# More of the start-up masks and all diagonal fills on GpSimd, the weight check moved behind the weights: a recurrent attention and its MLP on one core

## The chip, the cores and the metric

One core of one Trainium2 chip runs the kernel. The metric is the device time of one execution in microseconds (us). TensorE is called PE (PEld is its weight load), VectorE DVE, ScalarE ACT, GpSimd POOL and SyncE SP.

## The reference

There are 4 batches, 8 heads, 768 positions and a head size of 48. For each head a 48×48 state runs along the positions:

```python
cur = einsum('bhd,bhe->bhde', u[None] * kt, vt)
y[:, :, t] = einsum('bhd,bhde->bhe', rt, state + cur)
state = w[None, :, :, None] * state + einsum('bhd,bhe->bhde', kt, vt)
```

The outputs of all heads stand side by side as x (3072 tokens × 384) and go through an MLP of width 2048:

```python
h = x @ w_in
g = np.maximum(h, 0.0) + alpha * np.minimum(h, 0.0)
return g @ w_out
```

All inputs and the output are float32.

## The kernel before

**Tiling.** The positions are cut into 6 chunks of 128, so that a chunk has 512 tokens over the batches. Two heads make a pair, on partitions 0 to 47 and 64 to 111; there are 4 pairs. Inside a chunk the recurrence is written as products: r and k are scaled by tables of powers of w, scores are k against r under a strict triangular mask, the diagonal holds u·k·r, and what came before the chunk enters through the state. The MLP goes in main-loop steps: one step is one tile of 128 hidden columns of one chunk. `m_in` (L734) makes the hidden tile from x with 9 products (weights and x are each split into a high and a low float32r part, and three of the four combinations are taken, over 3 blocks of x), ACT and DVE make the activation and split it, and `m_out` (L760), 3 steps later, adds 9 products to the three output accumulators. There are 96 steps: 9 of chunk 0, 9 of chunk 1, the other 7 of each, then 16 of each later chunk.

**Start-up.** PE first runs 19 bf16 products on the identity (`warm`, L832 and L836), before any data is there. `first_chunk` (L437) handles the four pairs q of chunk 0, with tiles of the full 128 positions: DVE scales r and k (L447), makes their product (L533), PE sums it with u into the diagonal (`c_sum`, L540) and makes the scores (L457), DVE weighs v with the diagonal (L464), the scores are masked into `below`, and PE forms y (L485, L489, L498), which ACT copies out as the high part of x, PE subtracts (L508) and ACT copies again as the low part (L504). The mask of head g = 1 of a pair is a copy by ACT (L471) and a select by POOL (`affine_select`, L473); that of g = 0 is a DVE copy under a predicate (L477) onto a tile that POOL has cleared once (L268). The powers come from DVE (`table`, L275 to L279; L279 squares the last power into `w128`). `tokens_table` (L311) turns them into a table by tokens, `whalf`: ACT writes rows (L315), PE turns them (L322), DVE copies them (L325). With it DVE scales k of chunk 0 (L431) for the states (L521).

**Weights.** Each of the 16 weight tiles is loaded by SP (L334) and split by ACT and DVE (L359 to L378); the low part `wl` (L378) comes last, and a step needs both parts.

**Later chunks.** `burst` (L607) does a pair of chunks 1 to 5 with tiles of 64 positions: it makes scores and state products for one pair (L626, L633) and y for the pair before (L652 through the state, L662 through the scores). `prepare` (L553) loads and scales. There the tile `base` first gets the diagonal value `cu` on a 64×64 identity, for each of 2 heads and 4 batches (8 instructions per pair: in chunk 1 by POOL, L594, after that by ACT, L598), and then DVE copies the scores over it above the diagonal (L681). For chunks 2 to 5 `cu` comes from two POOL products (L582, L584) and a DVE sum (L588); for chunk 1 from PE (L540) and ACT (L546). L717 and L722 split y of chunk 1 by ACT and PE; L405 and L406 do it by ACT and DVE later.

**The check.** `check` (L808) tests that alpha is at most 1 and w lies within bounds, on DVE (L814 to L820), PE (L823) and DVE again (L825 to L829), and writes a flag that chooses, at the end, a general path which does not run here. Its rank is 40. All engines load the flag (L887).

**What sets the order.** Every instruction or small group is a `Piece` with an engine, a cost in us that is written into the code, the tiles that it reads and writes, and a rank. `in_order` (L93) plays the engines against these costs and picks, on the engine that is free first, the ready piece of the lowest rank; the resulting order is fixed when the program is built, and each engine runs its part strictly in that order. Scores, y and hidden tiles take turns in five PSUM banks, given out in that play. Where PE is idle in it ahead of the first step, filler `warm` products are written in front of the piece (L872 to L884). An SP load is costed by a shared transfer rate (L166).

## Time and profile before

| | |
|---|---|
| Three runs | 484.70, 484.49 and 485.74 us, median 484.7 us |
| The profiled execution | 485.77 us, of which the span from first to last instruction is 483.7 us |
| Granted TensorE clock, mean | 0.998 of full speed |
| DVE, ACT, POOL busy | 309.9, 244.8 and 98.4 us |
| Loaded from HBM | 37.17 MB |

Times in the views count from the start of the span. An engine's row gives the line of the code, the operation, the tiles written and read, and the count; a bracket tells how long the engine was idle before it and what ended that. PE's products are pipelined, so the busy time of one row runs into the next.

### The profile page before, as it was taken

The numbers are of one execution on the slowest core, as the hardware profiler recorded it, in microseconds if no ns is written. First come the engines' busy times: TensorE is split into PE (matmuls) and PEld (weight loads), VectorE is DVE, ScalarE is ACT, GpSimd is POOL, SyncE is SP. The second block draws the span as 40 slices with busy tenths as digits, with TensorE's granted clock in tenths as the row PEclk, the third lists the DMA queues.
The fourth block names the chain that finished last, engine by engine and source line by source line (L and its number), as shares of the span: only waits on it lengthen the run. The fifth ranks groups of instructions, "written<-read, shape, count | busy, mean of one in ns | idle before, by whom it ended". The sixth has DMA issues, their size and how long they took to land.

```text
span 483.7 us, 11271 instructions
## 1 busy us (share of the span) xinstructions
PE 473.4 (98%) x4667; PEld 385.5 (80%) x4667; DVE 309.9 (64%) x519; ACT 244.8 (51%) x554; POOL 98.4 (20%) x119
## 2 busy tenths in 40 slices
...
GB/s 220 284 228 184 250 248 170 214 147 51 54 160 122 211 96 59 149 88 37 88 54 37 151 89 35 72 56 1 119 1 1 1 1 0 66 0 1 0 0 71
DMA packets 23113, 46.22 MB, mean 96 GB/s; under 512 B 3376, under 2 KB 11184, under 8 KB 23056
## 3 DMA queue, kind: packets, MB, share of 16 engines
...
q8 instruction: 38, 0.62, 0.5%
q10 hardware_dynamic: 128, 0.23, 0.2%
q14 instruction: 19, 0.16, 0.1%
HBM read 37.17 MB, written 6.29 MB: 90 GB/s over the span
## 4 chain that ended last, share of the span: by engine, by line
PE 86%; DVE 5%; POOL 4%; ACT 2%; DMA 2%; issue 1%; ACTq 0%; DVEq 0%
PE acc L774 40%; PE bank L740 38%; POOL base L594 4%; PE bank L652 2%; PE bank L662 2%; PE bank L633 2%; PE bank L626 1%; DMA raw<-rk 1%; DVE raw L447 1%; ACT x L717 1%; DVE raw L565 1%; DMA wp<-wP 1%; DVE wl L378 1%; DVE kk L431 0%; DVE g L533 0%
## 5 line engine op out<-in xcount | busy, mean ns | idle before, releaser
L740 PE MATMUL bank<-x,wh 128*128 128x512 f32 x576 | 195.3, 392 | 0.0
L749 DVE SCALAR_TENSOR_TENSOR g<-bank,alph,g 128x512 f32<-128x512 f32 x96 | 71.9, 749 | 106.6 <-ACT g L748 106.5
L740 PEld LDWEIGHTS bank<-x,wh 128*128 128x128 f32 x576 | 108.1, 188 | 24.0 <-issue 0.8
L748 ACT ACTIVATE g<-bank 128x512 f32<-128x512 f32 x96 | 57.2, 596 | 129.2 <-PE bank L740 128.8
L740 PE MATMUL bank<-x,wl 128*128 128x512 f32 x288 | 112.2, 389 | 0.0
L752 ACT ACTIVATE gh<-g 128x512 fp32r<-128x512 f32 x96 | 60.5, 630 | 72.2 <-DVE g L749 72.1
L753 DVE TENSOR_TENSOR gl<-g,gh 128x512 fp32r<-128x512 f32 x96 | 72.4, 754 | 36.9 <-ACT gh L752 36.8
L774 PE MATMUL acc<-gh,wh 128*128 128x512 f32 x288 | 83.2, 396 | 0.0
L774 PE MATMUL acc<-gh,wl 128*128 128x512 f32 x288 | 81.6, 390 | 0.0
L774 PE MATMUL acc<-gl,wh 128*128 128x512 f32 x288 | 81.5, 390 | 0.0
L774 PEld LDWEIGHTS acc<-gh,wl 128*128 128x128 f32 x288 | 53.9, 188 | 11.4
L774 PEld LDWEIGHTS acc<-gl,wh 128*128 128x128 f32 x288 | 53.9, 188 | 11.3
L740 PEld LDWEIGHTS bank<-x,wl 128*128 128x128 f32 x288 | 54.1, 188 | 10.8
L774 PEld LDWEIGHTS acc<-gh,wh 128*128 128x128 f32 x288 | 52.7, 188 | 11.6 <-issue 0.4
L582 POOL TENSOR_TENSOR rr<-rr,kk 128x384 f32<-128x384 f32 x16 | 22.3, 1393 | 161.4 <-DMA kk<-vkr 93.6
L598 ACT ACTIVATE base<-ident,cu 128x64 f32<-128x64 f32 x128 | 32.9, 337 | 1.7 <-DVE cu L588 1.7
L594 POOL TENSOR_SCALAR base<-ident,cu 128x64 f32<-128x64 f32 x32 | 30.8, 984 | 13.7 <-ACT cu L546 13.7
L390 POOL DMA_DIRECT2D x<-x x30 | 15.4, 519 | 61.3 <-ACT o L801 49.4
L406 DVE TENSOR_TENSOR x<-bank,x 48x256 fp32r<-48x256 f32 x64 | 27.0, 422 | 1.3
L405 ACT ACTIVATE x<-bank 48x256 fp32r<-48x256 f32 x64 | 24.2, 379 | 2.1 <-PE bank L662 1.0
L568 DVE TENSOR_TENSOR raw<-raw,W 112x512 f32<-112x512 f32 x32 | 22.4, 723 | 2.2 <-DMA raw<-rk 2.2
L584 POOL TENSOR_TENSOR rr<-rr,utab 128x384 f32<-128x384 f32 x16 | 22.5, 1408 | 1.2
...
## 6 DMA issues: line engine op xcount, KB each, us to landing
...
```

The lines of the kernel that those rows point to most:

```text
L405: add("ACT", us, lambda: nc.scalar.activation(h(), view(), AF.Copy), r=[src], w=parts(x, 0, ps), rank=rank)
L406: add("DVE", us + 0.1, lambda: nc.vector.tensor_tensor(out=l(), in0=view(), in1=h(), op=ALU.subtract), r=[src] + parts(x, 0, ps), w=parts( ...
L568: add("DVE", 0.72, lambda t=t, tab=tab: nc.vector.tensor_tensor(out=t().rearrange("p b (j t) -> p (b j) t", j=2), in0=t().rearrange("p b ( ...
L584: add("POOL", 1.2, lambda: nc.gpsimd.tensor_tensor(out=rt().rearrange("p (g b) e -> p g b e", g=2), in0=rt().rearrange("p (g b) e -> p g b ...
L594: add("POOL", 1.0, lambda g=g, b=b: nc.gpsimd.tensor_scalar(base()[:, g, b], ident2(), cu()[:, g, b:b + 1], None, op0=ALU.mult), r=[cu, id ...
L598: add("ACT", 0.32, lambda g=g, b=b: nc.scalar.activation(base()[:, g, b], ident2(), AF.Copy, scale=cu()[:, g, b:b + 1]), r=[cu, ident2], w ...
L740: nc.tensor.matmul(hp()[:, :], a[i]()[:, k], X[c]()[:, x, k], start=(k == 0 and j == 0), stop=(k == NK - 1 and j == 2))
L748: add("ACT", 0.6, lambda: nc.scalar.activation(g(), hp()[:, :], AF.Copy), r=[hp], w=[g], rank=n - 100)
L749: add("DVE", 0.75, lambda: nc.vector.scalar_tensor_tensor(out=g(), in0=hp()[:, :], scalar=alph()[:, i:i + 1], in1=g(), op0=ALU.mult, op1=A ...
L752: add("ACT", 0.64, lambda: nc.scalar.activation(gh(), g(), AF.Copy), r=[g], w=[gh], rank=n - 100)
L753: add("DVE", 0.73, lambda: nc.vector.tensor_tensor(out=gl(), in0=g(), in1=gh(), op=ALU.subtract), r=[g, gh], w=[gl], rank=n - 99)
L774: nc.tensor.matmul(banks[k](), a[i]()[:, NK + k], x(), start=(begin and j == 0), stop=(end and j == 2))
```

## The change

The planner costs SP loads of under 16 KB at a fixed time, out of the shared rate. The masks of g = 0 for pairs 0 and 1 are done as those of g = 1, with a copy by ACT and a select by POOL, so the two clears of `below` go. The square of the last power moves from DVE to POOL. The first turn of the table by tokens gets rank −93 in place of −45. The diagonal of `base` is written, for all pairs of chunks 1 to 5, by two POOL selects, one for each half of the partitions: it takes the value of `cu`, read with step 0 along the position, where row and column agree, and 0 elsewhere. The check gets rank 24, and its first two DVE instructions name the last weight tile as an input. 22 warm products are written, and no filler follows directly behind them.

```diff
@@ -164,8 +164,11 @@
             if e == "POOL" and p.kb:
                 p.end += 3.0
             if e == "SP" or p.kb and e == "ACT":
-                dma = max(dma, p.end + 1.5) + p.kb / DMA_RATE
-                p.end = dma + 0.3
+                if p.kb < 16:
+                    p.end += 1.7
+                else:
+                    dma = max(dma, p.end + 1.5) + p.kb / DMA_RATE
+                    p.end = dma + 0.3
             done.append(p)
             for q in heirs.get(p, ()):
                 left[q] -= 1
@@ -263,9 +266,6 @@
     add("POOL", 0.1, lambda: nc.gpsimd.memset(uw(), 0.0), w=[uw], rank=-98)
     for i in range(2):
         add("POOL", 0.4, lambda i=i: nc.gpsimd.memset(weighed[i](), 0.0), w=[weighed[i]], rank=-95 + i)
-        for g in range(2):
-            if g == 0:
-                add("POOL", 0.4, lambda i=i, g=g: nc.gpsimd.memset(below[i][g](), 0.0), w=[below[i][g]], rank=-95 + i)
     for g in range(2):
         add("POOL", 0.25, lambda g=g: nc.gpsimd.tensor_tensor(
             out=uw()[half(g), :, g], in0=up()[half(g)], in1=wp()[half(g)], op=ALU.mult),
@@ -276,7 +276,7 @@
             out=t()[:, 64:129], data0=a()[:, m:m + 1].broadcast_to([112, 65]), data1=unit(), initial=0.0,
             op0=ALU.mult, op1=ALU.add), r=[wp, unit], w=[t], rank=10 * m - 95)
         add("DVE", 0.55, lambda: nc.vector.reciprocal(t()[:, 0:64], t()[:, 128:64:-1]), w=[t], rank=10 * m - 95)
-        add("DVE", 0.1, lambda: nc.vector.tensor_tensor(
+        add("POOL", 0.25, lambda: nc.gpsimd.tensor_tensor(
             out=w128()[:, m:m + 1], in0=t()[:, 128:129], in1=t()[:, 128:129], op=ALU.mult), r=[t], w=[(w128, m)],
             rank=10 * m - 78)
 
@@ -321,7 +321,7 @@
             for m in range(P):
                 nc.tensor.transpose(pt()[0:n, 128 * m:128 * m + 112], rows()[:, m, 0:n], ident()[0:112, 0:112])
 
-        add("PE", 0.6, turn, r=[rows, ident], w=[pt], rank=at)
+        add("PE", 0.6, turn, r=[rows, ident], w=[pt], rank=at - 48 * first)
         add("DVE", 0.4, lambda: nc.vector.tensor_copy(
             whalf()[0:n].rearrange("p (m g) e -> p m g e", g=2),
             pt()[0:n, :].rearrange("p (m g e) -> p m g e", m=P, g=2)[:, :, :, 0:D]), r=[pt], w=[whalf], rank=at)
@@ -467,12 +467,12 @@
             in1=bank()[:, 8 * q:8 * q + 8].rearrange("p (b g) -> p g b", g=2)[:, :, :, None].broadcast_to([128, 2, B, D]),
             op=ALU.mult), r=[(bank, q), v], w=[vc], rank=10 * q - 77)
         for g in range(2):
-            if g and True:
-                add("ACT", 0.6, lambda: nc.scalar.activation(
-                    base[1]().rearrange("p b t -> p (b t)"), A[1]()[:, :], AF.Copy), r=[A[1]], w=[base[1]], rank=q - 94)
-                add("POOL", 1.6, lambda: nc.gpsimd.affine_select(
-                    base[1](), base[1](), pattern=[[0, B], [1, L]], base=0, channel_multiplier=-1,
-                    compare_op=ALU.is_gt, fill=0.0), w=[base[1]], rank=q - 94)
+            if g or q < 2:
+                add("ACT", 0.6, lambda g=g: nc.scalar.activation(
+                    base[g]().rearrange("p b t -> p (b t)"), A[g]()[:, :], AF.Copy), r=[A[g]], w=[base[g]], rank=q - 94)
+                add("POOL", 0.75, lambda g=g: nc.gpsimd.affine_select(
+                    base[g](), base[g](), pattern=[[0, B], [1, L]], base=0, channel_multiplier=-1,
+                    compare_op=ALU.is_gt, fill=0.0), w=[base[g]], rank=q - 94)
                 continue
             add("DVE", 0.75, lambda g=g: nc.vector.copy_predicated(
                 base[g](), strict()[:, None, :].broadcast_to([128, B, L]),
@@ -588,16 +588,13 @@
             add("DVE", 0.55, lambda: nc.vector.tensor_reduce(
                 out=cu().rearrange("p g b -> p (g b)"), in_=rt(), axis=AX.X, op=ALU.add), r=[rt], w=[cu], rank=at - 1.8)
         base = sb([128, 2, B, HI], "base", 3)
-        for g in range(2):
-            for b in range(B):
-                if hasty:
-                    add("POOL", 1.0, lambda g=g, b=b: nc.gpsimd.tensor_scalar(
-                        base()[:, g, b], ident2(), cu()[:, g, b:b + 1], None, op0=ALU.mult), r=[cu, ident2],
-                        w=[(base, (g, b))], rank=at - 0.9)
-                    continue
-                add("ACT", 0.32, lambda g=g, b=b: nc.scalar.activation(
-                    base()[:, g, b], ident2(), AF.Copy, scale=cu()[:, g, b:b + 1]), r=[cu, ident2],
-                    w=[(base, (g, b))], rank=at - 0.9)
+        for j in range(2):
+            rows = slice(HI * j, HI * (j + 1))
+            add("POOL", 0.75, lambda rows=rows: nc.gpsimd.affine_select(
+                base()[rows].rearrange("p g b t -> p (g b) t"),
+                cu()[rows].rearrange("p g b -> p (g b)")[:, :, None].broadcast_to([HI, 2 * B, HI]),
+                pattern=[[0, 2 * B], [1, HI]], base=0, channel_multiplier=-1, compare_op=ALU.is_equal, fill=0.0),
+                r=[cu], w=[base], rank=at - 0.9)
         if hasty:
             by_tokens(k0, k, at - 3, at - 1.6)
         else:
@@ -809,11 +806,11 @@
 
         ok, w2, total = sb([128, NF + P + 1], "ok", 1), sb([112, P], "w2", 1), plan.buf(lambda: ok()[0:1, NF + P:])
         count = psum()
-        at = 40
+        at = 24
         add("POOL", 0.1, lambda: (ok(), w2(), nc.gpsimd.memset(ok()[:, 0:NF + P], 0.0)), w=[ok], rank=at)
-        add("DVE", 0.1, lambda: nc.vector.tensor_scalar(ok()[:, 0:NF], alph(), 1.0, None, op0=ALU.is_le), r=[alph],
+        add("DVE", 0.1, lambda: nc.vector.tensor_scalar(ok()[:, 0:NF], alph(), 1.0, None, op0=ALU.is_le), r=[alph, wl[NF - 1]],
             w=[ok], rank=at)
-        add("DVE", 0.1, lambda: nc.vector.tensor_tensor(out=w2(), in0=wp(), in1=wp(), op=ALU.mult), r=[wp], w=[w2],
+        add("DVE", 0.1, lambda: nc.vector.tensor_tensor(out=w2(), in0=wp(), in1=wp(), op=ALU.mult), r=[wp, wl[NF - 1]], w=[w2],
             rank=at)
         add("DVE", 0.1, lambda: nc.vector.tensor_scalar(ok()[0:112, NF:NF + P], w2(), 0.75 ** 2, None, op0=ALU.is_ge),
             r=[w2], w=[ok], rank=at)
@@ -833,7 +830,7 @@
         x = ident().bitcast(mybir.dt.bfloat16)
         nc.tensor.matmul(bank()[:, 256:512], x[:, 0:128], x, start=True, stop=True, skip_group_check=True)
 
-    add("PE", 4.0, lambda: [warm() for _ in range(19)], r=[ident], w=[(bank, "warm")], rank=-1000)
+    add("PE", 4.7, lambda: [warm() for _ in range(22)], r=[ident], w=[(bank, "warm")], rank=-1000)
 
     begins = {}
     for n, (c, i) in enumerate(STEPS):
@@ -856,7 +853,7 @@
     for n in range(NM):
         jobs.append((n, 6, lambda n=n: m_in(n)))
         jobs.append((n + MLAG - 0.5, 5, lambda n=n: m_out(n)))
-    jobs.append((40, 7, check))
+    jobs.append((24, 7, check))
 
     for m in range(P):
         table(m)
@@ -876,7 +873,8 @@
             if any(x is acc_of[0] for x, _ in p.uses):
                 break
             step = p.rank >= 0 and p.us == 0.7
-            fill[p], last = 0 if last is None else int(max(0.0, p.start - last - 0.05) / (0.25 if step else 0.125)), p.end
+            fill[p] = 0 if last is None else int(max(0.0, p.start - last - 0.05) / (0.25 if step else 0.125))
+            last = p.end if p.rank > -1000 else None
     with tc.manual_schedule():
         for p in order:
             for _ in range(fill.get(p, 0)):
```

## Rows read from the trace of the kernel before

**Rows 1.** The page, part 1: busy time and share of the span of each engine
```profile
PE 473.4 (98%) x4667; PEld 385.5 (80%) x4667; DVE 309.9 (64%) x519; ACT 244.8 (51%) x554; POOL 98.4 (20%) x119
```

**Rows 2.** Windows: length; busy us PE, PEld, DVE, ACT, POOL; clock, DMA share, GB/s
```profile
15.00:20.00 5.00, 5.00 (x72) 3.88 (x71) 4.93 (x12) 5.00 (x15) 1.00 (x2) 1.00 1.05 350
40.00:45.00 5.00, 4.66 (x114) 3.73 (x115) 4.66 (x10) 2.73 (x6) 5.00 (x5) 1.00 0.48 135
100.00:150.00 50.00, 50.00 (x517) 41.27 (x516) 42.73 (x68) 29.89 (x77) 13.10 (x10) 1.00 0.38 119
```

**Rows 3.** Chain that ended last, first 100 us, two pieces: start, us, what
```profile
33.96 9.16 POOL base L594 x8
53.56 8.38 POOL base L594 x8
```

**Rows 4.** Waits of PE, 26 to 81 us, all of them: total, times, longest
```profile
PE bank L652 <- ACT x L717: 0.7, 1, 0.7
PE bank L652 <- DVE base L681: 0.3, 1, 0.3
PE bank L540 <- DVE g L533: 0.2, 1, 0.2
PE bank L303 <- DVE raw L565: 0.2, 1, 0.2
```

**Rows 5.** Timeline of PE, to 31 us: start, us, line, op, tiles, count, idle before
```profile
1.46 5.09 PE L834 MATMUL acc<-ident 128*128 128x256 bf16 x23 [1.46 <-POOL ident L249]
13.25 1.16 PE L457 MATMUL bank<-raw 48*128 48x128 f32 x16 [0.19 <-DVE raw L447]
23.37 0.74 PE L498 MATMUL bank<-x,pick 112*128 112x512 f32 x2
26.06 0.48 PE L740 MATMUL bank<-x,wh 128*128 128x512 f32 x1
30.69 0.82 PE L834 MATMUL acc<-ident 128*128 128x256 bf16 x6
```

**Rows 6.** Timeline of DVE, 8 to 42 us, chosen rows
```profile
8.85 1.14 DVE L533 TENSOR_TENSOR g<-raw 112x512 f32<-112x512 f32 x1
10.38 0.73 DVE L477 COPY_PREDICATED below<-strict,bank 128x512 f32<-128x512 uint8 x1
11.90 1.29 DVE L447 TENSOR_TENSOR raw<-raw,W 112x512 f32<-112x512 f32 x2
13.11 0.15 DVE L279 TENSOR_TENSOR w<-W 112x1 f32<-112x1 f32 x1
...
21.99 0.17 DVE L814 TENSOR_SCALAR ok<-alph 128x16 f32<-128x16 f32 x1
...
30.70 0.95 DVE L378 TENSOR_TENSOR wl<-wx,wh 128x768 fp32r<-128x768 f32 x1
41.49 0.16 DVE L825 TENSOR_REDUCE ok<-bank 1x1 f32<-1x20 f32 x1
```

**Rows 7.** Timeline of POOL, 8.8 us
```profile
8.81 0.64 POOL L473 TENSOR_SCALAR_AFFINE_SELECT below<-below 128x512 f32<-128x512 f32 x1 [2.78 <-ACT below L471]
```

**Rows 8.** Instructions of one line: ns shortest/median/longest, first and last start
```profile
L533 DVE TENSOR_TENSOR g<-raw x7: 683/693/1137, 6.0 to 54.4; 112x512 f32<-112x512 f32 x7
L594 POOL TENSOR_SCALAR base<-ident,cu x32: 433/442/4077, 34.0 to 66.1; 128x64 f32<-128x64 f32 x32
```

**Rows 9.** Groups by line: count | busy us, mean ns of one | idle before
```profile
L598 ACT ACTIVATE base<-ident,cu 128x64 f32<-128x64 f32 x128 | 32.9, 337 | 1.7 <-DVE cu L588 1.7
L471 ACT ACTIVATE gl<-acc 128x512 f32<-128x512 f32 x2 | 1.2, 592 | 1.8 <-PE acc L457 1.8
L473 POOL TENSOR_SCALAR_AFFINE_SELECT below<-below 128x512 f32<-128x512 f32 x2 | 1.3, 636 | 6.2 <-ACT below L471 6.2
```

**Rows 10.** Waits of DVE, 26 to 81 us, the longest one
```profile
DVE base L681 <- POOL base L594: 1.6, 4, 0.8
```

**Rows 11.** The flag's load on SP, by its line: ns, first and last start
```profile
L887 SPq TENSOR_LOAD <-flag x1: 492/492/492, 42.5 to 42.5; - x1
```

## The prediction

> **What bounds the kernel now.** I read the page's busy shares first: PE is busy 98% of the span [rows 1], and in the windows it fills its stretch completely from 100 us on (50.00 of 50 us) while DVE has room (42.73) [rows 2]. So behind the start-up the end is set by the length of PE's queue, and work taken from ACT or POOL there buys nothing. The chain that ended last tells another story for the first 100 us: two blocks of POOL's diagonal fills (L594), 9.16 and 8.38 us, stand in it [rows 3]. Those 17.5 us are not to be had. The chain follows the releaser that came last, also while PE has other work in its queue: in the list of what PE waited for between 26 and 81 us there are 1.4 us in all, 0.7 + 0.3 of them at L652, the first products of a burst, behind those fills [rows 4]. Over that stretch PE does main-loop steps as the weights come, attention bursts in between, and filler products.
>
> Before 26.06 us, where the first main-loop product starts [rows 5], DVE is the busiest of the vector engines (4.93 of 5 us at 15 to 20 us, and still 4.66 at 40 to 45) [rows 2]. PE's third scores product at 13.25 us waits for DVE's scaling of r and k that starts at 11.90 [rows 5, 6]; after that PE is full up to the last of x at 23.37 us (5.00 of 5) [rows 2, 5], and then comes a fixed tail of two copies by ACT and one correction by PE up to 26.06. So time is won in three places alone: an earlier 13.25, PE's waits and fillers between 26 and 81 us, or that tail.
>
> **The change, part by part.** Sums are made against the profiled execution (485.77 us, span 483.7); the median of the three runs, 484.7, lies 1.1 us lower, so I apply the difference to the median.
>
> *Masks of pairs 0 and 1.* Two selective copies by DVE (0.73 each, L477) [rows 6] go; ACT gets two copies (0.59 each) and POOL two selects (0.64 each) more [rows 9] (the first select, at 8.81 us, found POOL idle for 2.78 us [rows 7]). Removed from DVE: 2 × 0.73 = 1.46 us, of which one lies ahead of the scaling at 11.90. Two 0.5 us clears of POOL in the first 4 us go with them; nothing waited for those.
>
> *Square of the last power (L279).* Four times 0.15 us leave DVE [rows 6] for POOL, whose small instructions stand behind at most two selects; first users are ACT's rows for the table. 0.6 us of DVE removed, one or two of the four ahead of 11.90 or the next scaling.
>
> *Check behind the weights.* Four small instructions at 21.99 us (at most 4 × 0.17 = 0.68) and three at 41.49 (3 × 0.16 = 0.48) [rows 6] leave the full stretch for some 130 us, where DVE has 7 us of room in 50 [rows 2]; if that room were gone they would cost 1.2 us of DVE, not of PE. Between the two groups the check also holds one of the five rotating PSUM banks, until 41.49 us; that is freed. The flag's load sits in SP's queue right behind the check (42.5 us, 0.49 us) [rows 11] and moves with it; queued behind it on SP are input loads for bursts, which the code ranks seven main-loop steps ahead of their burst, so a wait of a few us there stays hidden, and PE would be the one to wait if not.
>
> *Table turned early.* The transposes get a rank ahead of the remaining first-chunk products. Neither they nor the copy and the four scalings of k behind them get shorter; they come sooner, so the state products can fill the tail ahead of 26.06. But the turn stands in PE's in-order queue: if ACT's rows for it are late, the x products behind it wait. Bounds: from −0.5 (wait) to +0.5 us (the filler and idle time of the tail).
>
> *Warm-up.* 23 products ran at the start, 19 written and 4 as filler, in 5.09 us, 0.22 each [rows 5]; 22 remain, as the filler behind them goes. At most 0.2 us of PE, ahead of a DVE-paced stretch: I take 0.
>
> These four together move the first main-loop product: DVE is eased by 0.73 + 0.15 us ahead of 11.90, but the new selects can take some back, see below. I take 0.5 us, bounds −0.5 and +1.2.
>
> *Diagonal fills of chunk 1.* Eight POOL instructions per pair become two selects. An L594 takes 0.44 us at the median but up to 4.08 [rows 8], and eight took 8.4 to 9.2 us [rows 3]. A fill reads a broadcast column and writes 512 numbers per partition, on half the partitions; the nearest row is the 512-element select at 0.64 [rows 9], upper bound the excess that L594 shows per piece on top: (9.16 − 8 × 0.44) / 8 = 0.7, so 1.3 each. A pair takes 1.3 to 2.7 us in place of 8 to 9. That removes the two waits of PE at L652 and 1.6 us in which DVE stood idle for the fills [rows 10]. Gain on PE: 1.0, bounds 0 (the 0.7 is released by a copy of ACT, which may be late for its own reasons) and 1.4, all of PE's waits.
>
> *Filler and weights.* At 30.69 us PE runs six filler products, 0.82 us [rows 5], and then waits 0.2 for DVE [rows 4]; the second weight tile is only finished by DVE at 31.65 (30.70 + 0.95) [rows 6]. DVE ahead by some 2 us (1.46 + 0.6 + 0.68 = 2.7, less collisions) has it done as the first step ends. Gain 0.6, bounds 0 and 1.1: the fillers are written from the planner's gaps, not from the chip's.
>
> *Diagonal fills of later chunks.* 128 ACT instructions (32.9 us in total) [rows 9] become 32 selects, 20.5 us on POOL at 0.64. POOL is at 13.10 of 50 us there [rows 2]. A select waits for its pair's reduction; queued behind it are the next pair's two POOL products and DMA issues, and the next burst needs the mask about four steps later. At 0, bounds −0.3 and +0.3; if POOL's cover were gone, one late mask would cost PE its wait per burst.
>
> The planner's new price for small loads only reorders them; 0. Sum: 0.5 + 1.0 + 0.6 = 2.1 us: 483.7 for that execution, **482.6** against the median. All lower ends together give 0.8 us lost, all upper ends 4.0 won.
>
> **Row against rule.** DVE's product at 8.85 us took 1.14 us where its kind takes 0.69, and a select had started on POOL 0.04 us before [rows 6 to 8]: 0.44 lost. The other way round, L594's longest pieces stand in full DVE stretches. The Trainium skill, SBUF — State Buffer, section "Who interferes with whom", says that a DVE instruction with two SBUF inputs and a GpSimd instruction that reads SBUF exclude each other for a whole instruction, whoever starts first. The trace agrees with that in this one pair of rows. By it, a select costs DVE up to its full length; by the row 0.44 us, and only where it meets such an instruction.
>
> **The rivals.** *The selects take back what they free.* Ten new selects (two masks, eight fills) run in the stretch where DVE is full. If each blocks a two-input instruction for its whole 0.64 us, DVE loses 6.4 us against 1.46 + 0.6 + 0.68 + 0.48 + 1.6 = 4.8 freed; the weights come 1.6 us later and PE, which starts each of the first steps as its weights arrive, with them: 484.7 + 1.6 = 486.3. It decides from the eighth collision on (4.8 / 0.64 = 7.5). For it: the row at 8.85. Against it: at 0.44 ten collisions cost 4.4, and the 32 instructions that go collided too. The rule above is what this rival rests on.
>
> *Little moves.* The selects of pair 1 fall on the scaling at 11.90, so that the first step stays at 26.06; the 0.7 us wait for ACT remains; gain 0.3 + 0.6 = 0.9: 483.8. For it: PE's queue was full in nearly the whole stretch, so a shorter chain beside it counts for nothing.
>
> *All covers fall at once.* With the bank freed and DVE ahead, the planner packs first chunk and first steps tightly and every term reaches its upper end: 4.0 won, 480.7. Against it: each of these is a separate wait.
>
> **How the numbers follow.** About 0.3% (1.45 us) can be told from no change. The forecast (1.5 to 3.3 us won) gets 0.55, the upper ends 0.07, little moves 0.27, the selects taking it back 0.11. So faster 0.62, same 0.27, slower 0.11. The range goes from 480.6, the upper ends, to 485.3, just short of the lower ends together (485.5); it leaves out the blocking rival's full price and a little at either side.
>
> **What would show it.** Right: the first L740 at 25 to 26 us; no filler near 30 us; PE's waits between 26 and 81 us below 0.5 us; the fills at L594 as selects of 0.6 to 1.3 us and gone from the chain; ACT some 33 us less busy with no gain behind 100 us, where the distance between steps stays as it was. Wrong: selects over 2 us each, two-input DVE instructions of over 1 us around them with the weights' last step (L378) later than now, PE waiting at the turned table or at L489, SP standing long at the flag's load, or new waits at L662 in the later bursts.

## The result, and the profile after

The changed kernel takes 487.79 us (median of 8 runs, 485.59 to 490.27) against 484.93 us (8 runs, 484.49 to 485.74) in the same runs: ratio 1.0058, 95% interval 1.0034 to 1.0081, so 2.9 us slower. (Ratios leave out runs far above a kernel's fastest, which the medians below keep, so that a ratio can differ from the quotient of two medians.) The profiled execution happens to be the fastest of the eight: 485.59 us, span 483.5, against 485.77 and 483.7 before. So the best run of the changed kernel is set beside a run at the slow end of the kernel before. Two facts already lie in these numbers: the best run is 0.7 us above the median of the kernel before and inside its range, and the others lie up to 4.7 us above that best run.

The page, part 1, answers to [rows 1]:

```profile
PE 471.3 (97%) x4650; PEld 383.7 (79%) x4650; DVE 306.5 (63%) x513; ACT 215.9 (45%) x428; POOL 110.2 (23%) x131
```

ACT has lost 28.9 us, POOL has got 11.8 and DVE lost 3.4, as the change says. None of it is time won, so I followed PE instead: the start of the n-th main-loop product (L740 and L774 before, L737 and L771 after, 1728 in all) in the one trace minus that in the other.

| product | before, us | after, us | difference |
|---|---|---|---|
| 1st | 26.06 | 26.18 | +0.1 |
| 217th | 97.85 | 94.77 | -3.1 |
| 352nd | 131.83 | 131.76 | -0.1 |
| last | | | +0.3 |

So 3.1 us were won in the start-up, more than the 2.1 forecast, kept up to 126 us and lost again within 5 us. The waits of PE from 26 to 81 us, all of them, answer to [rows 4], where they were 1.4 us:

```profile
PE bank L649 <- ACT cu L546: 0.2, 1, 0.2
```

And those from 100 to 160 us, where the kernel before has none:

```profile
PE bank L649 <- DVE g L746: 1.7, 1, 1.7
PE bank L659 <- ACT seen_y L672: 0.8, 1, 0.8
```

That is 2.5 of the 3.0 us lost there. The timeline of PE shows where (start, us, line, tiles, count, idle before):

```profile
126.77 0.32 PE L649 MATMUL bank<-raw,T 48*48 48x64 f32 x4
128.76 0.59 PE L649 MATMUL bank<-raw,T 48*48 48x64 f32 x26 [1.67 <-DVE g L746]
...
131.38 0.44 PE L659 MATMUL bank<-base,v 64*48 64x64 f32 x16 [0.81 <-ACT seen_y L672]
```

PE stands in the middle of an attention burst, for the PSUM bank that L746 is to read out. (L746 is DVE's part of the activation g; the expectations call it the accumulation, and so does this text.) The timeline of DVE at that place, after:

```profile
125.29 0.69 DVE L750 TENSOR_TENSOR gl<-g,gh 128x512 fp32r<-128x512 f32 x1 [0.70 <-ACT gh L749]
127.48 0.56 DVE L431 TENSOR_TENSOR kk<-kk,whalf 128x384 f32<-128x384 f32 x1 [1.50 <-POOL rr L582]
127.96 0.74 DVE L746 SCALAR_TENSOR_TENSOR g<-bank,alph,g 128x512 f32<-128x512 f32 x1
```

and the same instructions before (L749 is the accumulation there):

```profile
126.91 0.69 DVE L753 TENSOR_TENSOR gl<-g,gh 128x512 fp32r<-128x512 f32 x1 [0.70 <-ACT gh L752]
127.52 0.74 DVE L749 SCALAR_TENSOR_TENSOR g<-bank,alph,g 128x512 f32<-128x512 f32 x1
129.11 0.56 DVE L431 TENSOR_TENSOR kk<-kk,whalf 128x384 f32<-128x384 f32 x1 [0.84 <-POOL rr L582]
```

The planner has written the two in the other order. Before, the accumulation stood ahead of the scaling of k (L431), and DVE's wait for POOL's product rr fell behind it; now DVE stands 1.50 us for POOL with the accumulation that PE needs queued behind. Why is POOL's rr not 3.1 us earlier too, as PE is? The timeline of POOL after:

```profile
100.00 4.50 POOL L593 TENSOR_SCALAR_AFFINE_SELECT base<-cu 64x512 f32<-64x512 f32 x2 [32.06 <-DVE cu L588]
104.59 1.80 POOL L582 TENSOR_TENSOR rr<-rr,kk 128x384 f32<-128x384 f32 x1
...
126.45 1.00 POOL L582 TENSOR_TENSOR rr<-rr,kk 128x384 f32<-128x384 f32 x1 [4.57 <-DMA rr<-vkr]
```

and before:

```profile
105.25 1.02 POOL L582 TENSOR_TENSOR rr<-rr,kk 128x384 f32<-128x384 f32 x1 [32.10 <-DVE wx L374]
...
128.05 1.02 POOL L582 TENSOR_TENSOR rr<-rr,kk 128x384 f32<-128x384 f32 x1 [3.98 <-DMA rr<-vkr]
```

The product starts 0.7 us earlier than before at 105 us and 1.6 us earlier at 128 us, where PE is 3.1 us earlier. At the first of these places two selects, 4.50 us together, stand ahead of it in POOL's queue. They run in this window (length; busy us of PE, PEld, DVE, ACT, POOL; granted clock; DMA share; GB/s), in which DVE is busy for 4.96 of 5 us:

```profile
100.00:105.00 5.00, 5.00 (x24) 4.14 (x23) 4.96 (x7) 2.63 (x5) 4.85 (x3) 1.00 0.50 143
```

The selects by their line (ns shortest, median, longest) answer to [rows 8]:

```profile
L593 POOL TENSOR_SCALAR_AFFINE_SELECT base<-cu x40: 651/1068/3182, 31.6 to 343.0; 64x512 f32<-64x512 f32 x40
```

The pairs of a chunk share one rr buffer: a pair's load (L580) is issued after the reduction (L588) of the pair ahead has read it. It is a chain through SP, DMA, POOL and DVE, and it has its own lead.

The other 2 us of the median are not in this profile. The mean granted clock of the eight runs goes from 0.985 to 0.997, of the kernel before's, in all its runs here, from 0.994 to 0.999 but for one at 0.557 (787.79 us); this profile is the 0.997.

### The profile page after: what moved, and what is told of

It reads as the page before. It is cut to its first block, busy times and chain, and to the rows that moved or that the text cites. A ratio compares the mean times of both kernels' runs of the same rounds, so it can differ in the third digit from the quotient of the medians.

```text
span 483.5 us, 11133 instructions
## 1 busy us (share of the span) xinstructions
PE 471.3 (97%) x4650; PEld 383.7 (79%) x4650; DVE 306.5 (63%) x513; ACT 215.9 (45%) x428; POOL 110.2 (23%) x131
## 4 chain that ended last, share of the span: by engine, by line
PE 81%; DVE 7%; DMA 3%; ACT 3%; issue 2%; POOL 2%; SPq 1%; ACTq 0%; DVEq 0%; POOLq 0%
PE acc L771 37%; PE bank L737 35%; PE bank L649 2%; PE bank L659 2%; DMA wraw<-wall 2%; PE bank L630 2%; PE bank L623 1%; DMA raw<-rk 1%; DVE wx L374 1%; DVE gl L750 1%; POOL base L593 1%; DVE wl L378 1%; ACT wh L377 1%; DVE g L746 1%; ACT x L714 1%
## 5 line engine op out<-in xcount | busy, mean ns | idle before, releaser
L737 PE MATMUL bank<-x,wh 128*128 128x512 f32 x576 | 195.1, 392 | 0.0
L746 DVE SCALAR_TENSOR_TENSOR g<-bank,alph,g 128x512 f32<-128x512 f32 x96 | 71.9, 749 | 108.5 <-ACT g L745 107.0
L737 PEld LDWEIGHTS bank<-x,wh 128*128 128x128 f32 x576 | 108.1, 188 | 23.6 <-issue 0.8
L737 PE MATMUL bank<-x,wl 128*128 128x512 f32 x288 | 112.3, 390 | 0.0
L749 ACT ACTIVATE gh<-g 128x512 fp32r<-128x512 f32 x96 | 60.6, 632 | 78.2 <-DVE g L746 78.0
L750 DVE TENSOR_TENSOR gl<-g,gh 128x512 fp32r<-128x512 f32 x96 | 71.9, 749 | 36.6 <-ACT gh L749 36.5
L771 PE MATMUL acc<-gh,wh 128*128 128x512 f32 x288 | 83.4, 397 | 0.0
L771 PE MATMUL acc<-gh,wl 128*128 128x512 f32 x288 | 81.9, 391 | 0.0
L771 PE MATMUL acc<-gl,wh 128*128 128x512 f32 x288 | 81.5, 390 | 0.0
L593 POOL TENSOR_SCALAR_AFFINE_SELECT base<-cu 64x512 f32<-64x512 f32 x40 | 40.0, 999 | 180.5 <-PE bank L659 119.1
L737 PEld LDWEIGHTS bank<-x,wl 128*128 128x128 f32 x288 | 54.1, 188 | 11.2 <-DVE wl L378 0.4
L771 PEld LDWEIGHTS acc<-gl,wh 128*128 128x128 f32 x288 | 53.9, 188 | 11.3
L771 PEld LDWEIGHTS acc<-gh,wl 128*128 128x128 f32 x288 | 53.7, 188 | 11.5
L771 PEld LDWEIGHTS acc<-gh,wh 128*128 128x128 f32 x288 | 52.6, 188 | 11.4
L568 DVE TENSOR_TENSOR raw<-raw,W 112x512 f32<-112x512 f32 x32 | 21.0, 684 | 2.8 <-DMA raw<-rk 2.8
L678 DVE COPY_PREDICATED base<-strict,bank 128x256 f32<-128x256 uint8 x40 | 15.7, 441 | 4.9 <-PE bank L630 3.9
```

What stands on the lines that cost most here:

```text
L568: add("DVE", 0.72, lambda t=t, tab=tab: nc.vector.tensor_tensor(out=t().rearrange("p b (j t) -> p (b j) t", j=2), in0=t().rearrange("p b ( ...
L593: add("POOL", 0.75, lambda rows=rows: nc.gpsimd.affine_select(base()[rows].rearrange("p g b t -> p (g b) t"), cu()[rows].rearrange("p g b ...
L737: nc.tensor.matmul(hp()[:, :], a[i]()[:, k], X[c]()[:, x, k], start=(k == 0 and j == 0), stop=(k == NK - 1 and j == 2))
L746: add("DVE", 0.75, lambda: nc.vector.scalar_tensor_tensor(out=g(), in0=hp()[:, :], scalar=alph()[:, i:i + 1], in1=g(), op0=ALU.mult, op1=A ...
L749: add("ACT", 0.64, lambda: nc.scalar.activation(gh(), g(), AF.Copy), r=[g], w=[gh], rank=n - 100)
L750: add("DVE", 0.73, lambda: nc.vector.tensor_tensor(out=gl(), in0=g(), in1=gh(), op=ALU.subtract), r=[g, gh], w=[gl], rank=n - 99)
```

## The experiments

Theories, as the expectations name them: **S**, the selects of chunks 2 to 5 hold up POOL's rr chain; **S'**, they lengthen DVE's two-input instructions there; **C**, the check; **W**, without filler products the clock falls in the start; **P**, the stand-still near 127 us lets it fall again; **R**, the one rr buffer; **O**, DVE's fixed order; **M** and **T**, masks or table won the start. Where a run is of one kernel on another, its planner writes that kernel's order anew. The results in one table; leads are as in the table above (minus: ahead of the kernel before), from the one profiled execution of each. The expectations count products from 0, so their 351 is the 352nd here. Among the profiles with no fall of the clock in the start, the first product lies +0.1 to +1.2 us, so leads of different kernels are told apart from about 1 us on. All of them are taken against one profile of the kernel before, 0.8 us above the median of its eight runs.

| run | median us (runs) | ratio, 95% interval | 1st | 217th | 352nd | last | clock of the runs |
|---|---|---|---|---|---|---|---|
| e1_after_again | 488.07 (6) | 1.0056, 1.0037 to 1.0075 | +1.8 | -0.4 | +2.9 | +3.3 | 0.989 to 0.993 |
| e2_act_late | 489.72 (8) | 1.0049, 1.0018 to 1.0079 | +2.8 | +0.4 | +2.8 | +3.2 | 0.975 to 0.998 |
| e3_warm30 | 496.31 (6) | 1.0234, 1.0221 to 1.0248 | +4.1 | +2.2 | +6.8 | +7.1 | 0.977 to 0.986 |
| e4_check_back | 487.92 (5) | 1.0067, 1.0052 to 1.0082 | +1.8 | -0.6 | +2.6 | +2.6 | 0.989 to 0.993 |
| e5_fill | 487.28 (7) | 1.0060, 1.0038 to 1.0083 | +0.5 | -2.8 | +1.1 | +1.8 | 0.988 to 0.993 |
| e6_rr2 | 487.90 (7) | 1.0047, 1.0027 to 1.0066 | +3.7 | +0.7 | +2.8 | +3.2 | 0.975 to 0.996 |
| e7_fill_rr2 | 485.53 (11) | 1.0006, 0.9997 to 1.0015 | +0.7 | -2.4 | -0.2 | +0.1 | 0.995 to 0.999 |
| e8_before_nofill | 485.97 (13) | 1.0019, 1.0005 to 1.0032 | +7.5 | +7.3 | +7.3 | +7.3 | 0.977 to 0.997 |
| e9_fill_order | 485.06 (11) | 1.0002, 0.9991 to 1.0014 | +1.0 | -2.5 | -0.8 | -0.4 | 0.994 to 0.999 |
| e10_fill_c1back | 489.51 (6) | 1.0092, 1.0079 to 1.0105 | +0.2 | -3.0 | +0.9 | +1.2 | 0.988 to 0.996 |
| e11_fill_check70 | 487.90 (6) | 1.0047, 1.0033 to 1.0061 | +1.1 | -2.0 | +2.0 | +2.3 | 0.968 to 0.996 |
| e12_combined | 484.15 (12) | 0.9983, 0.9973 to 0.9993 | +1.0 | -2.1 | -1.2 | -0.8 | 0.995 to 0.998 |
| e13_fill_masks | 484.77 (10) | 0.9988, 0.9974 to 1.0001 | +1.2 | -1.4 | -0.1 | +0.2 | 0.991 to 0.998, one 0.655 |
| e14_fill_table | 490.01 (4) | 1.0104, 1.0083 to 1.0125 | +1.0 | +1.4 | +4.0 | +4.3 | 0.993 to 0.998 |
| e15_combined_check | 485.46 (12) | 1.0016, 1.0000 to 1.0033 | +0.7 | -1.0 | -0.3 | -0.3 | 0.993 to 0.998 |
| **e16_order_check** | **483.24 (8)** | **0.9967, 0.9951 to 0.9983** | +1.0 | -2.0 | -2.0 | -2.0 | 0.993 to 0.999 |
| e17_order_selects | 485.26 (11) | 1.0000, 0.9988 to 1.0012 | +0.9 | -1.9 | +0.1 | +0.5 | 0.994 to 0.999 |
| e18_check_only | 489.12 (6) | 1.0082, 1.0049 to 1.0115 | +0.7 | -1.8 | +2.5 | +4.8 | 0.986 to 0.996 |

### The clock: e1, e3, e8, e5

**e1_after_again**, the changed kernel once more, with no edit.

> The changed kernel itself, for a second profile. In its first profile PE is 3.1 us ahead of the kernel before from the sixth step on, stands still at 126.8 us (1.7 us) and 130.3 us (0.8 us), and ends level; the other runs took 1 to 5 us longer at a lower mean clock. Theory S (the gain is given back in chunk 2, where the pairs go one by one through a single r tile): PE stands still at the same two places, 2 to 3 us in all. Theory W (the start is less even without the 17 filler products that the kernel before ran between its first scores and its first step): the record of the clock shows it rising late or falling inside the first 15 us. Theory P (the stand-still near 127 us lets the clock fall): the record shows half speed for 3 us or more behind 127 us, in a run that takes over 487 us. Time 485.5 to 490.

It came out as before (1.0056), and this profile has a fall of the clock. Windows of the start (columns as above), first of the profile of the change, then of e1:

```profile
8.00:12.00 4.00, 3.39 (x52) 2.76 (x52) 3.81 (x8) 1.45 (x3) 3.77 (x6) 1.00 1.06 261
12.00:16.00 4.00, 3.57 (x54) 2.94 (x53) 3.90 (x7) 2.89 (x9) 1.44 (x2) 1.00 1.03 346
```

```profile
8.00:12.00 4.00, 2.76 (x39) 2.23 (x41) 3.97 (x7) 1.17 (x3) 3.18 (x5) 0.91 1.05 235
12.00:16.00 4.00, 4.00 (x45) 3.26 (x43) 3.90 (x7) 1.20 (x3) 1.05 (x2) 0.66 1.06 323
```

The longest wait of PE in the start of e1:

```profile
PE acc L457 <- DVE raw L447: 1.4, 1, 1.4
```

In e1 PE waited 1.4 us for the scaled r and k in the first of the windows, and then the clock went from 2.4 to 1.2 GHz for part of the two windows: 4 x 0.09 + 4 x 0.34 = 1.7 us of full-speed time gone. The first main-loop product is 1.7 us later than in the other profile of the same kernel (+1.8 against +0.1), and everything behind it with it. So W is seen here, and S in that PE stands 1.9 and 0.8 us at the same two places. P is not: the clock stays up behind them.

**e3_warm30**: 30 warm products at the very start.

```diff
-    add("PE", 4.7, lambda: [warm() for _ in range(22)], ...
+    add("PE", 6.38, lambda: [warm() for _ in range(30)], ...
```

> 30 warm products in place of 22, all else as changed. They last until about 8 us and so delay the first scores by up to 1.7 us, a cost of at most 1.7 us. Theory W: the clock stays up once it has risen, every run has 0.996 or more, and the times lie within 1 us of each other, at 485 to 487. Theory P: the spread stays (1 to 5 us over the fastest) and the mean clock still varies between 0.985 and 0.997.

The worst run of all, where W had forecast 485 to 487: the clock rose in time and fell again at 12 us, at the end of a wait of 1.6 us, then once more near 135 us, behind the stand-still. More work ahead of the gaps didn't help here; e5 below fills the gaps themselves.

**e8_before_nofill**: the kernel before with 22 warm products and no filler.

```diff
-    ... [warm() for _ in range(19)] ...
+    ... [warm() for _ in range(22)] ...
...
-            for _ in range(fill.get(p, 0)):
-                warm()
             p.fn()
```

> The kernel before without any filler product (22 at the start, then none; before had 23 and 16 more). Theory W: the clock falls again inside the first 16 us in most runs, mean clock 0.985 to 0.994, the times scatter over 2 us or more and the median is 1.5 to 4 us slower than before, 486.5 to 489. Rival: the clock stays, and the time is that of before within 0.5 us, or up to 0.5 us faster for the 0.8 us of filler at 30 us.

Windows of its profiled execution:

```profile
8.00:12.00 4.00, 3.25 (x44) 2.74 (x42) 3.93 (x8) 0.91 (x2) 1.27 (x2) 0.78 1.05 297
12.00:16.00 4.00, 4.00 (x33) 3.26 (x32) 3.93 (x9) 0.60 (x1) 0.00 (x0) 0.50 1.03 388
16.00:26.00 10.00, 10.00 (x77) 7.49 (x76) 4.95 (x10) 6.78 (x18) 1.30 (x2) 0.50 0.52 157
```

A longer fall on the old kernel, with nothing changed but the fillers and three more warm products at the start: the first product comes 7.5 us later in this execution. It is one of three, of 13, that took over 492 us and that the ratio leaves out. Of the other ten, four have a mean clock of 0.988 to 0.992 and take 485.9 to 487.5 us, and the fastest takes 484.1. So W holds on the kernel before too, in some of its executions, but it costs less than forecast: the ratio is 1.0019 and the median 485.97, below the 486.5 to 489 expected.

**e5_fill**: the changed kernel with 6 fillers ahead of the second scores product and 3 ahead of the third. The kernel before has six and two at these places, and none is left in the changed kernel. They read, before:

```profile
8.52 0.83 PE L834 MATMUL acc<-ident 128*128 128x256 bf16 x6
12.67 0.39 PE L834 MATMUL acc<-ident 128*128 128x256 bf16 x2
```

```diff
+            if p.us == 1.1:
+                scores_seen = scores_seen + 1
+                fill[p] = max(fill[p], (0, 6, 3, 0)[scores_seen - 1])
```

> The changed kernel with nine filler products more: 6 ahead of the second scores and 3 ahead of the third, about where the kernel before had 6 and 2. Theory W (the clock falls in the start because PE does too little between 6 and 15 us): the clock rises once and stays, every run has 0.995 or more, the times lie within 1.2 us of each other, at 485.0 to 486.2, which is the changed kernel's best run; the stand-still near 127 us stays. Rival (the clock's fall depends on the moment of the start alone): as the changed kernel, 486 to 490 with clocks of 0.985 to 0.997.

No fall in the start, and the lead is there, 2.8 us. Of the six profiles of the changed kernel and its variants without these fillers (the first, e1 to e4, e6) all but the first have a fall in the start; of the twelve with them none has. Yet W's forecast of 0.995 in every run failed: all seven have 0.988 to 0.993, and the median is only 0.5 us below that of the change. Near 127 us PE waits:

```profile
PE bank L649 <- DVE g L746: 2.3, 1, 2.3
```

and the window there (columns as above) reads:

```profile
126.00:134.00 8.00, 5.68 (x137) 4.77 (x136) 4.78 (x10) 4.19 (x10) 3.14 (x4) 0.79 0.36 114
```

2.3 us of waiting, and behind it the lower clock: 8 x 0.21 = 1.7 us; together 4.0, where the leads of -2.8 and +1.1 lie 3.9 us apart. That is P, in its own rows. So the stand-still costs 1.7 times what the list of waits shows, in an execution in which the clock falls behind it.

### What makes PE stand: e2, e4, e6, e7, e9

**e2_act_late**: the fills of chunks 2 to 5 back to eight ACT instructions a pair, chunk 1 with selects.

```diff
-        for j in range(2):
+        for j in range(2 if hasty else 0):
...
+        for g in range(0 if hasty else 2):
+            for b in range(B):
+                add("ACT", 0.32, lambda g=g, b=b: nc.scalar.activation(
+                    base()[:, g, b], ident2(), AF.Copy, scale=cu()[:, g, b:b + 1]), ...
```

> The diagonal fills of chunks 2 to 5 go back to ACT, 8 per pair; those of chunk 1 stay two selects. Theory S: without two selects of 1.0 us each between the sum of one pair and the products of the next on POOL, the chain of chunk 2 runs 1 to 3 us earlier, PE's stand-still at 127 to 131 us falls from 2.5 us to under 1, and the time is 482.5 to 484. Rival C (the check, now at 122 us on DVE and as a wait of SP for its flag, causes it): the stand-still stays over 2 us, time as the changed kernel, 485.5 to 490. Theory P: with the stand-still gone, all runs have a mean clock of 0.997; theory W: the clock still varies between 0.985 and 0.997.

The stall shrank, from 2.5 to 1.9 us of waits, between the two forecasts (under 1 for S, over 2 for C), and did not go; the clock fell in the start too. I took S for fallen. That was too early: e17 below shows S at work behind O.

**e4_check_back**: the check at its old rank, without the weights as inputs.

```diff
-        at = 24
+        at = 40
...
-        add("DVE", 0.1, lambda: ..., r=[alph, wl[NF - 1]], ...
+        add("DVE", 0.1, lambda: ..., r=[alph], ...
...
-    jobs.append((24, 7, check))
+    jobs.append((40, 7, check))
```

> The check goes back to its place of before (rank 40, no wait for the last weight tile). Rival C: the stand-still near 127 us goes or falls below 1 us and SP waits 0.4 instead of 4.1 us for the flag; time 483 to 485. Theory S: the stand-still at 127 to 131 us stays at 2 to 3 us, and the start loses up to 0.7 us of DVE; time 485.5 to 490.

The stall stays (1.6 + 0.8 us), so the check is not its cause. The step of 0.36 us near 152 us is gone. By the timeline it isn't the flag's load but the check's own PE products (L820, 150.50 us in the profile of the change), which now stand in PE's full queue and before stood at a place where PE had time.

**e6_rr2** and **e7_fill_rr2**: two rr buffers (the unused tile `pad` makes room), without and with the fillers of e5.

```diff
-    fixed([128, 128], "pad")
...
-            rt = sb([128, 2 * B, D], "rr", 1)
+            rt = sb([128, 2 * B, D], "rr", 2)
```

> The changed kernel with two buffers for the r tile of chunks 2 to 5 in place of one (an unused 512-byte tile is left out to make room). Theory R (the last scaling of k in chunk 2 waits on DVE for a POOL product that waits for the load of that tile, whose only buffer the pair before still holds; an activation of the main loop stands behind it on DVE and keeps a bank from PE): the wait of DVE for POOL at that scaling falls from 1.5 us to under 0.4, PE's stand-still at 127 to 131 us from 2.5 us to under 1; the time falls by 2 to 3 us against the changed kernel, with the same spread from the start: 483 to 487. Rival (PE runs into the weights or the main loop's activations there, whatever the tile): stand-still and time stay, 485.5 to 490.

> Both edits: the nine filler products and the two r tiles. Theories W and R together: 482.2 to 483.5 in every run, 1.5 to 2.5 us faster than the kernel before, that is by what the start gained. If only W holds 485 to 486.2; if only R, a spread of 483 to 487.

In both PE waits 0.8 + 0.4 us in place of 2.5. Without fillers that isn't seen in the time (487.90 us, where 483 to 487 was expected). With fillers the clock is 0.995 or more in all 11 runs and the time level with the kernel before. So with two buffers PE no longer stands long enough for the fall, but 2.2 of the lead's 2.4 us are given back all the same: R and W together, forecast at 482.2 to 483.5, missed by 2 us. DVE's order is written anew here too, so this isn't R alone.

**e9_fill_order**: e5 with one instruction moved. L431 of that pair is given the accumulation as an input, which moves it two places back in DVE's order; PE's, ACT's and POOL's orders are the same.

```diff
-            add("DVE", 0.56, lambda: scale_k(k, whalf, q), r=[whalf], w=[k], rank=at - 1.6)
+            add("DVE", 0.56, lambda: scale_k(k, whalf, q), r=[whalf] + ([g_of[19]] if (c, q) == (3, 0) else []), w=[k], rank=at - 1.6)
...
-        gs[n] = gh, gl
+        gs[n], g_of[n] = (gh, gl), g
```

> The changed kernel with the filler products of e5_fill and one instruction moved: VectorE's scaling L431 of the first pair of chunk 3 is held back until the accumulation L746 that stands behind it has been done, so it stands two places later in VectorE's order; every other engine's order is the same as in e5_fill. Theory O (the stand-still near 127 us is VectorE's fixed order: L431 waits for GpSimd's rr, and the accumulation that frees TensorE's bank stands behind it): TensorE's wait of 2.3 us for the accumulation near 128 us falls under 1 us, the clock does not fall at 130 us, the lead of 2.7 us over the kernel before is 2 us or more at product 351, and the time is 482.5 to 484.5. Rival B (VectorE is full there whatever the order): the wait moves to the next accumulations, the lead at product 351 is under 1 us, and the time stays at 485 or above.

PE's waits, 100 to 160 us:

```profile
PE bank L659 <- ACT seen_y L672: 0.8, 1, 0.8
PE bank L649 <- DVE g L746: 0.4, 1, 0.4
```

From 2.3 to 0.4 us at the accumulation, no fall of the clock, 487.28 to 485.06 us. O holds for 2.2 us, half a microsecond short of the time forecast; most of the lead (-2.5 to -0.8) is still lost, so that lead and time come out as for the rival, in which DVE is full there whatever its order.

### Where the start's gain came from: e10, e13, e14

Each is e5 with one part of the change undone.

**e10_fill_c1back**: chunk 1's diagonals by eight POOL multiplications a pair.

```diff
-        for j in range(2):
+        for j in range(0 if hasty else 2):
...
+        for g in range(2 if hasty else 0):
+            for b in range(B):
+                add("POOL", 1.0, lambda g=g, b=b: nc.gpsimd.tensor_scalar(
+                    base()[:, g, b], ident2(), cu()[:, g, b:b + 1], None, op0=ALU.mult), ...
```

> The kernel of e5_fill with the diagonals of chunk 1 written by 8 GpSimd multiplications for a pair again, as in the kernel before; later chunks keep the selects. If the selects of chunk 1 gave the start's gain, the lead over the kernel before at products 162 to 324 shrinks from 2.7 us by 1.5 to 2.5 us; if it came from the masks, the earlier table and the missing check of alpha, it shrinks by under 0.5 us. By both, the stand-still near 127 us stays or grows with a smaller lead, so the end is at or above that of e5_fill.

The lead is 3.0 against 2.8 us: the selects of chunk 1 gave nothing to it that these profiles can tell. The stall is there (2.2 + 0.8 us). Why its median is 2.2 us above e5's I can't say from one profile.

**e13_fill_masks**: the masks of pairs 0 and 1 on DVE again (and POOL's two clears).

```diff
-            if g or q < 2:
+            if g:
```

> The kernel of e5_fill with the masks of the first head of pairs 0 and 1 done by VectorE's selective copies again (and the two clears of below), as in the kernel before. Theory M (the start's gain of 2.8 to 3.0 us at products 162 to 324 comes from VectorE's relief by these two copies, 1.5 us): the lead there shrinks by 1.0 us or more, to under 1.9 us. Rival T (it comes from the table turned early): it shrinks by under 0.5 us. The stand-still near 127 us is as in e5_fill or smaller by what the lead loses.

The lead is 1.4 us, 1.4 less, of which 0.6 is the first product. M holds, hardly clear of the 1 us of the caveat. But the time is 484.77 us, 2.5 us below that of e5, which has twice the lead. The planner has here written DVE's order as in the kernel before (L749 is the accumulation, L434 the scaling of k):

```profile
127.91 0.75 DVE L749 SCALAR_TENSOR_TENSOR g<-bank,alph,g 128x512 f32<-128x512 f32 x1
129.35 0.69 DVE L753 TENSOR_TENSOR gl<-g,gh 128x512 fp32r<-128x512 f32 x1 [0.70 <-ACT gh L752]
130.94 0.56 DVE L434 TENSOR_TENSOR kk<-kk,whalf 128x384 f32<-128x384 f32 x1 [0.90 <-POOL rr L585]
```

PE doesn't wait for the accumulation and the clock doesn't fall. Of the runs that take back or alter one part (e2, e4, e10, e11, e13, e14) only this one has that order.

**e14_fill_table**: the turn of the table at its old rank.

```diff
-        add("PE", 0.6, turn, r=[rows, ident], w=[pt], rank=at - 48 * first)
+        add("PE", 0.6, turn, r=[rows, ident], w=[pt], rank=at)
```

> The kernel of e5_fill with the first turn of the table by tokens back at its old rank. Theory T (the early turn lets the state products fill the tail ahead of the first main-loop product): the lead at products 162 to 324 shrinks by 1.0 us or more, from 2.8 us. Rival M (the masks gave it): it shrinks by under 0.5 us.

The lead of 2.8 us becomes 1.4 us behind: 4.2 us, the largest of the parts. T holds, and so does M; the parts don't add up to 2.8, as each undoing has the whole start planned anew. And though PE is behind the kernel before here, it stands 1.3 and 0.8 us at the same two places and loses 2.6 us more: the loss there doesn't need a lead. In the profile of the change, PE's timeline (to be set beside [rows 5]) shows how the table works:

```profile
23.63 1.13 PE L521 MATMUL bank<-v,kk 128*64 128x48 f32 x32
...
25.13 0.67 PE L521 MATMUL bank<-v,kk 128*64 128x48 f32 x16
25.80 0.60 PE L303 MATMUL bank<-ident,raw 112*128 112x112 f32 x4
26.18 0.48 PE L737 MATMUL bank<-x,wh 128*128 128x512 f32 x1
```

and in the kernel before, behind its first product at 26.06:

```profile
26.94 1.93 PE L521 MATMUL bank<-v,kk 128*64 128x48 f32 x48
```

The state products L521 need k scaled by the table. Turned early, 48 of the 64 run ahead of the first main-loop product in place of none. That product comes no sooner, but 1.9 us of work less stand behind it, and with the six fillers (0.82) and the wait behind them (0.2) [rows 4, 5] gone the sum is 3.0 us; from the 1st to the 28th product PE draws 2.9 us ahead.

### Keeping the gain: e11, e12, e15 to e18

**e11_fill_check70**: e5 with the check's rank 70.

```diff
-        at = 24
+        at = 70
...
-    jobs.append((24, 7, check))
+    jobs.append((70, 7, check))
```

> The kernel of e5_fill with the check of alpha moved behind step 70 of the main loop, beyond the stretch in which VectorE is full. Theory C' (the check's VectorE work adds to that stretch and its flag load costs 0.36 us near 152 us): the step of 0.36 us near 152 us goes, and the lead at product 351 grows by at most 0.6 us, to a time of 486.3 to 487. If the check costs nothing, the time is that of e5_fill. TensorE's wait of 2.3 us for the accumulation stays in both.

The step near 152 us goes and comes back later (+0.3 at the end); the four DVE instructions stay behind the weights. Nothing won.

**e12_combined**: e5 with two rr buffers, ACT's fills in chunks 2 to 5, the check at rank 70. **e15_combined_check**: the same with the check as before (e4's edit in place of e11's). Both are made of edits shown above:

```diff
-            rt = sb([128, 2 * B, D], "rr", 1)
+            rt = sb([128, 2 * B, D], "rr", 2)
...
-        for j in range(2):
+        for j in range(2 if hasty else 0):
```

> All that looked useful together: the filler products of e5_fill, two rr buffers (the unused tile pad makes room), the diagonals of chunks 2 to 5 on ScalarE as in the kernel before, the check of alpha behind step 70. If the selects of the later chunks are what stretches VectorE's two-input operations between 105 and 131 us (theory S'), the lead of 2.4 us lasts to the end and the time is 482.2 to 483.5. If VectorE is full there without them too, the lead at product 351 is under 0.8 us and the time is 484.3 to 485.5.

> e12_combined with alpha's check where the kernel before has it. Theory C2 (the four instructions of the check at 124 us, 0.55 us of VectorE just ahead of the waits near 127 us, and the flag's load later on cost what was left): the lead of 2.06 us at products 162 to 324 is 1.5 us or more at product 351, nothing is lost behind that, and the time is 483.2 to 483.9. If the check is not what matters, the lead at 351 is 1.2 us or less and the time 484.0 to 484.5.

e12 is the first to beat the kernel before, by 0.2%, but gives back 0.9 of its 2.1 us by the 352nd product, and its time lies between its two forecasts. e15 missed both of its own, by 1 us and more: the lead at product 352 is that of "not what matters", the time is above either. It doesn't settle the matter, as e15 has a wait of 1.5 us for L750 at 67 us that e12 doesn't have. From the 217th to the 352nd product e15 loses 0.7 us and e12 0.9, so the check's place there made little difference.

**e16_order_check**: e9 with ACT's fills in chunks 2 to 5 and the check as before, one rr buffer (the edits of e5, e9, e2 and e4).

```diff
-            add("DVE", 0.56, lambda: scale_k(k, whalf, q), r=[whalf], ...
+            add("DVE", 0.56, lambda: scale_k(k, whalf, q), r=[whalf] + ([g_of[19]] if (c, q) == (3, 0) else []), ...
...
-        for j in range(2):
+        for j in range(2 if hasty else 0):
```

> e9_fill_order with the check where the kernel before has it and the diagonals of chunks 2 to 5 on ScalarE, one rr buffer. If the one rr buffer is harmless once the order is mended, it does as e15: 483.2 to 483.9. If VectorE's waits for GpSimd through rr still cost, the lead at product 351 is under 1 us, and the time 484.3 to 485.3.

483.24 us, 0.33% (0.17 to 0.49) below the kernel before: the lead of 2.0 us is there at the last product to the hundredth, and PE waits for nothing between 100 and 160 us. That is the forecast for a harmless buffer (483.2 to 483.9). DVE in the same place (L751 is the accumulation here):

```profile
125.52 0.75 DVE L751 SCALAR_TENSOR_TENSOR g<-bank,alph,g 128x512 f32<-128x512 f32 x1
127.87 0.56 DVE L431 TENSOR_TENSOR kk<-kk,whalf 128x384 f32<-128x384 f32 x1 [1.60 <-POOL rr L582]
```

DVE still waits 1.60 us for POOL, but with nothing urgent behind it. The one buffer is harmless so.

**e17_order_selects** differs from e16 by selects in all chunks. **e18_check_only** differs from e17 by the two places of one instruction. As edits of e16, and then of e17:

```diff
-        for j in range(2 if hasty else 0):
+        for j in range(2):
...
-            ... r=[whalf] + ([g_of[19]] if (c, q) == (3, 0) else []), ...
+            ... r=[whalf], ...
```

> e16_order_check with the selects of the changed kernel in all chunks, instead of ScalarE's fills in chunks 2 to 5. If these selects are harmless once VectorE's order is right, the lead of some 2 us stays past product 351 to the end and the time is that of e16, 483.0 to 483.8. If they stretch VectorE's work enough to be felt (theory S'), the lead at product 351 is under 1.2 us and the time 484.0 to 485.0.

> e17 without the moved instruction: the changed kernel with its filler products and the check where the kernel before has it, VectorE's own order. Theory O: TensorE waits over 1 us for the accumulation near 127 us, the clock falls there in part of the runs, and the time is 486 to 487.5. If the check's four instructions were the cause and not the order, the lead stays past product 351 and the time is 483 to 484.5.

e18 against e17 is O once more: 3.9 us for two places, 1.6 us more than the forecast's upper end, with a wait of 2.3 us and behind it the lower clock, 8 x 0.43 = 3.4 us in this execution:

```profile
132.00:140.00 8.00, 7.33 (x90) 5.82 (x81) 5.35 (x12) 3.80 (x10) 1.94 (x2) 0.57 0.77 226
```

e17 against e16 is the price of the selects, together with the order that the planner writes for them, as DVE's queue changes too: the lead of 1.9 us is gone at product 352, and the time is 2.0 us longer by the medians, 1.6 by the ratios (0.3 us above what was forecast for S'). POOL in e17:

```profile
101.11 6.19 POOL L593 TENSOR_SCALAR_AFFINE_SELECT base<-cu 64x512 f32<-64x512 f32 x2 [31.60 <-DVE cu L588]
107.38 1.02 POOL L582 TENSOR_TENSOR rr<-rr,kk 128x384 f32<-128x384 f32 x1
...
129.25 1.01 POOL L582 TENSOR_TENSOR rr<-rr,kk 128x384 f32<-128x384 f32 x1 [4.54 <-DMA rr<-vkr]
```

and in e16:

```profile
103.26 1.01 POOL L582 TENSOR_TENSOR rr<-rr,kk 128x384 f32<-128x384 f32 x1 [33.87 <-DVE wx L374]
...
126.82 1.01 POOL L582 TENSOR_TENSOR rr<-rr,kk 128x384 f32<-128x384 f32 x1 [4.74 <-DMA rr<-vkr]
```

Two selects take 6.19 us, the next pair's rr product stands behind them, and the chain is 4.1 us later at once and 2.4 us later at the fourth pair. POOL is busy for 19.41 of the 29 us from 101 to 130 us, against 10.76 in e16, so it still has room; what is short is not POOL but its place in the order. DVE pays for it at the reduction, in e17 and then in e16:

```profile
109.53 0.55 DVE L588 TENSOR_REDUCE cu<-rr 128x8 f32<-128x384 f32 x1 [2.75 <-POOL rr L584]
```

```profile
107.38 0.54 DVE L588 TENSOR_REDUCE cu<-rr 128x8 f32<-128x384 f32 x1
```

That stand-still of 2.75 us is S. The longer DVE instructions of S' are the smaller part: from 100 to 129 us all DVE instructions together take 3.7 us more than the shortest of their kind in e17, and 2.8 us in e16.

## Why the prediction was wrong

**What bounds the kernel.** Right as to PE's queue and the start, and the start gave 3.1 us in the profile of the change (2.8 in e5) where 2.1 were forecast. Wrong was the sentence drawn from it, that behind the start-up the end is set by the length of PE's queue. It held for the kernel before: its serial rr chain (load, two POOL products, DVE's reduction) kept DVE waiting 0.84 us at 129 us with nothing urgent behind, and I never asked how late it stood. With the selects in that chain and DVE's order changed PE loses 3.0 us there. The lead isn't what brings this on: e14 loses 2.6 us from behind the kernel before, and e16, without the selects of the later chunks and with the order mended, keeps its 2.0 us.

**Diagonal fills of later chunks, at 0 with bounds of 0.3.** This is a step that failed. The prediction saw that "queued behind it are the next pair's two POOL products and DMA issues" and then priced the selects by 0.64 us each and POOL's share of the stretch. In DVE's full stretch a pair of selects took 4.50 and 6.19 us, and the price is 1.6 to 2.0 us (e17 against e16), not the 0.3 at most.

**"The distance between steps stays as it was."** Also failed: the planner wrote DVE's order anew, two instructions changed places at 127 us, and that alone is worth 2.2 us (e9 against e5) to 3.9 us (e17 against e18). An edit that touches a planner's inputs changes orders far from the edit; the prediction said that of the price of small loads alone, and at 0. Which edit of the change did it is open in part: with the masks back on DVE the old order returns (e13), with the check, the table or the selects of some chunks undone it doesn't.

**Warm-up, "I take 0".** Failed: the four fillers behind the warm products and those among the first scores go with the change, and the prediction counted fillers as PE time and never as what keeps the clock. Without them the granted clock falls in the start in many runs (e1, where it cost 1.7 us; e8), and behind the stand-still at 127 us it can fall once more (1.7 us in e5, 3.4 in e18). The spread of the eight runs, from 485.6 us at a mean clock of 0.997 to 490.3 at 0.985, goes with the clock, and so do 2.2 of the 2.9 us of the median's distance. That it is these two falls in each of the eight is likely and not shown, as one of them alone has a profile; neither profile of the changed kernel has the second fall.

**Table turned early, bounds of -0.5 and +0.5.** Mis-sized: the direction and the mechanism ("the state products can fill the tail") were right, but the fill was priced by the idle time of the tail and not by the 1.9 us of work drawn ahead. Undone it costs some 4 us of lead (e14).

**Masks, and 0.5 us for the first product.** The first product did not move (+0.1), yet DVE's relief counts in the lead, up to 1.4 us by e13. **Diagonal fills of chunk 1, 1.0.** Nothing (e10): the waits at L652 went, but they are gone in e10 too, with the old fills. **Filler and weights, 0.6.** Near its upper bound: 0.8 us of fillers and 0.2 of waiting gone. That wait was misread, though: it is L540's, for DVE's product at L533, and not one for the weights.

**The check, "1.2 us of DVE, not of PE".** Its product on PE was forgotten: 0.36 us, as soon as it stands in PE's full queue.

**The rivals.** "The selects take back what they free" named the time nearest to the measured one (486.3), by collisions in the start that would delay the weights. It came out otherwise, so the nearness is luck: the weights came earlier (the last step of the second tile, in place of 30.70 us [rows 6]),

```profile
27.74 0.95 DVE L378 TENSOR_TENSOR wl<-wx,wh 128x768 fp32r<-128x768 f32 x1
```

and the collisions that cost time struck at 100 us, with POOL as the one that is held up. There the trace agrees with the rule weighed in the prediction (the Trainium skill, SBUF — State Buffer, "Who interferes with whom": a DVE instruction with two SBUF inputs and a reading GpSimd instruction shut each other out): a pair of selects that would take 1.3 us by its shortest took 4.50 us while DVE was busy for 4.96 of 5 us. I had used that rule in one direction only, for what DVE loses. Of the signs that the prediction set itself, those of the start came true but for the first product at 26.18 us (no filler near 30 us, 0.2 us of waits of PE between 26 and 81 us), and so did two of being wrong: selects over 2 us, and a new wait of 0.8 us in a later burst (L659, L662 before).
